# Attention-value products that load 128 stationary columns instead of 96

## The chip, the cores and the metric

One core of a Trainium2 chip runs the whole program. The metric is the time of one execution in device microseconds; lower is better. PE is TensorE, PEld its weight load, DVE is VectorE, ACT is ScalarE, POOL is GpSimd. Times are medians over several executions, and each experiment was timed in five rounds beside the kernel before on the same chip.

## The reference, cut to what matters

An attention layer is followed by an MLP. For each of 4 batches and 8 heads the sequence of 768 is cut into 8 blocks of 96. A doubly normalised 8x8 matrix mixes the blocks of k and v, then each block of q attends to its own mixed block:

```python
scores = scale * np.matmul(q_b, k_sb.transpose(0, 1, 2, 4, 3))   # 96 x 96 per head and block
scores = scores - np.max(scores, axis=-1, keepdims=True)
attn = np.exp(scores)
attn = attn / (np.sum(attn, axis=-1, keepdims=True) + 1e-09)
return np.matmul(attn, v_sb).reshape(B, H, S, D)                 # 96 x 96 times 96 x 64
...
tok = np.einsum('ts,bsd->btd', w_tok, a1)                        # 768 x 768 token product
u = x + lam * tok
ch = np.maximum(a2 @ w_ch1, 0.0) @ w_ch2                         # 512 -> 2048 -> 512
```

The change is in the last product of the attention, `attn @ v`. There are 4 x 8 x 8 = 256 of them, each with 96 rows of attention, 96 keys and 64 values, plus one column of ones in v that yields the row sums.

## The kernel before

The exponentials of a pair of heads and four blocks lie side by side in one tile `et`: 96 partitions (keys) by 2 x 4 x 96 columns (queries). The 96 query columns of one block are the stationary operand of a product; the 65 columns of `Vs` stream past. `et` is written by one ACT instruction:

```python
        et = att.tile([BLK, 2, 4, BLK], F16, name="et", tag="et", bufs=4)      # BLK = 96
        act.activation(et[:]..., sps[0:BLK]..., AF.Exp, scale=scale)
```

Batches 1 to 3 use `emit_pv`, and the scheduler mixes its products with those of the MLP of the batch before:

```python
    def emit_pv(b, h4, ets, x128, xs):
        for g in range(2):
            xps = psa([BLK, 4, 256], FT, "x_ps")
            for ii in range(4):
                i = 4 * g + ii
                for h2 in range(2):
                    pe.matmul(
                        xps[:, ii, h2 * GRP:h2 * GRP + D + 1], ets[g][:, h2, ii, :],
                        Vs[b % NV][:, (2 * h4 + h2) * NB + i, 0:D + 1],
                        start=True, stop=True,
                    )
            ...                             # DVE: reciprocal of the sums, multiply, into x128
```

Batch 0 uses `pv_tiles`, in a fixed order. Three blocks fill output rows 0 to 95 and thirds of a fourth block (32 columns each) fill rows 96 to 127, so that the token product can contract over 128 rows:

```python
        for rows, cols, i in ((slice(0, BLK), BLK, 0), (slice(BLK, 128), 32, 3)):
            for h2 in range(2):
                for ii in range(3):
                    vi = 3 * g + ii if i == 0 else 6 + g
                    lhsT = et[:, h2, ii, :] if i == 0 else et[:, h2, 3, 32 * ii:32 * ii + 32]
                    pe.matmul(xps[rows, h2, ii, 0:D + 1], lhsT, Vs[0][...], start=True, stop=True)
```

So 240 products load 96 columns (48 in batch 0, 192 later), and 48 load 32.

The softmax here doesn't subtract the row's maximum and nothing guards it: scores larger than these inputs give would overflow.

## Time and profile before

| | before |
|---|---|
| time, median (lowest to highest) | 271.24 us (271.13 to 271.33) |
| span of the profiled execution | 269.4 us |
| PE busy | 97% |
| attention-value products (x_ps) in the chain that ended last | 5.6% |
| start to start of a 96-column product, median of 240 | 45 ns |

The first lines are from the page of the kernel before: its part 1 (busy microseconds, share of the span, instructions) and two rows of part 2 (tenths busy, and granted clock in tenths, in 40 slices of the span).

```profile
PE 260.8 (97%) x2049; PEld 145.5 (54%) x2059; DVE 155.0 (58%) x333; ACT 126.0 (47%) x232; POOL 92.4 (34%) x100
...
PE   7899999999999999999999999999999999999993
...
PEclk9999999999999999999999999999999999999999
```

TensorE is busy from end to end at full clock. A busy PE is not yet a PE at its peak, because the ends of products are modelled. What a product costs is read from where the next one starts. The chain of waits that ended last, in order of time, gives this for whole groups of products (start, microseconds, what). Three of its lines from a later attention stretch of the kernel before:

```profile
130.88 0.71 PE x_ps L65 x16
131.59 1.30 PE h_ps L65 x8
...
140.06 0.35 PE x_ps L65 x8
```

Sixteen attention-value products take 0.71 us and eight take 0.35, about 44 ns each. Eight products of the MLP (128 stationary, 384 moving columns) take 1.30 us, 162 ns each. The groups of instructions by shape show the weight loads (PEld). After the bar stand busy microseconds and the mean duration of one in ns:

```profile
L65 PEld LDWEIGHTS <-W1p 128*128 128x128 bf16 x512 | 47.6, 98 | 30.3 <-issue 0.9
...
L65 PEld LDWEIGHTS <-et 96*96 96x96 f16 x240 | 14.3, 125 | 3.1 <-issue 0.3
```

The load of 96 columns lasts 125 ns and the larger load of 128 columns 98 ns. The duration includes latency that overlaps with other loads. The spacing of products has to be taken from the starts of single records. Over the whole trace, products with 128 stationary columns start 56, 162 and 216 ns apart for 128, 384 and 512 moving columns (medians): 0.417 ns per moving column plus 2.5. A product with 65 moving columns would then need 29.6 ns, and 45 ns were measured. Here the load is the longer of the two.

### The profile page before, as it was taken

Reading aid. Unit: us, or ns where it says so; the run is one execution under the profiler, and the core shown is the slowest. Engines: PE = TensorE matmul, PEld = TensorE weight load, DVE = VectorE, ACT = ScalarE, POOL = GpSimd, SP = SyncE. Lnnn points to the kernel's source line nnn. Section 1 sums busy time; section 2 is a strip of 40 time slices with the busy share of each in tenths; the row PEclk is TensorE's granted clock in tenths of the full one; section 3 lists DMA queues with packets and bytes.
Section 4 is the critical chain, followed back from the end, with each engine's and each line's share of the span. In section 5 each row is a group of like instructions: output and inputs, shape, how many; then the busy total and the mean of one; then the engine's idle time right before and its main releaser. Section 6 shows DMA issues by size and latency. Waiting matters only on the chain.

```text
span 269.4 us, 5147 instructions
## 1 busy us (share of the span) xinstructions
PE 260.8 (97%) x2049; PEld 145.5 (54%) x2059; DVE 155.0 (58%) x333; ACT 126.0 (47%) x232; POOL 92.4 (34%) x100
## 2 busy tenths in 40 slices
PE   7899999999999999999999999999999999999993
PEld 2467755565566444554565444654665445545542
DVE  6878688639567876722575966714575962042033
ACT  3376757642585312980365414970475305604600
POOL 8524689103574624007917225002409000000000
PEclk9999999999999999999999999999999999999999
DMA  6999999989999543499999342493200332012012
GB/s 80 181 208 249 207 211 207 210 197 113 193 171 163 106 93 97 117 83 83 208 202 137 61 99 79 117 104 55 79 2 2 78 78 78 2 39 78 2 39 78
DMA packets 62423, 30.88 MB, mean 115 GB/s; under 512 B 48888, under 2 KB 58112, under 8 KB 62400
## 3 DMA queue, kind: packets, MB, share of 16 engines
q0 software_dynamic: 23024, 15.60, 39.0%
q1 hardware_dynamic: 39376, 14.96, 33.4%
q8 instruction: 16, 0.26, 0.4%
q14 instruction: 7, 0.06, 0.1%
HBM read 32.78 MB, written 8.65 MB: 154 GB/s over the span
## 4 chain that ended last, share of the span: by engine, by line
PE 89%; ACT 4%; DVE 4%; issue 1%; DMA 1%; DVEq 0%; ACTq 0%
PE ch_ps L65 30%; PE h_ps L65 30%; PE tok_ps L65 12%; PE x_ps L65 6%; PE sc_ps L65 4%; ACT kT L65 2%; PE v_ps L65 2%; PE k_ps L65 1%; PE q_ps L65 1%; ACT et L65 1%; DVE csum L65 1%; DVE P_78 L65 1%; PE m_ps L65 1%; DVE rsum L65 1%; PE wtok_ps L65 1%
## 5 line engine op out<-in xcount | busy, mean ns | idle before, releaser
L65 ACT ACTIVATE hTa<-h_ps 128x384 bf16<-128x384 f32 x96 | 45.9, 492 | 70.9 <-PE h_ps L65 70.0
L65 PE MATMUL ch_ps<-W2p,hTa 128*128 128x512 bf16 (+2 forms) x290 | 66.0, 371 | 0.5
L65 PEld LDWEIGHTS <-W1p 128*128 128x128 bf16 x512 | 47.6, 98 | 30.3 <-issue 0.9
L65 DVE TENSOR_TENSOR ch_ps<-ch_ps,lamB 128x512 f32<-128x512 f32 (+2 forms) x25 | 16.9, 677 | 64.3 <-PE ch_ps L65 61.7
L65 PEld LDWEIGHTS <-hTa 128*128 128x128 bf16 x300 | 28.6, 98 | 32.4
L65 ACT ACTIVATE et<-sc_ps 96x768 f16<-96x768 f32 x32 | 24.9, 807 | 12.1 <-PE sc_ps L65 12.1
L65 PE MATMUL ch_ps<-W2p,hTb 128*128 128x512 bf16 (+2 forms) x100 | 25.0, 371 | 0.0
L65 PEld LDWEIGHTS <-w_tokT 128*128 128x128 f16 x180 | 14.8, 97 | 16.1
L65 DVE TENSOR_TENSOR tok_ps<-tok_ps,a1lB 128x512 f32<-128x512 f32 x24 | 16.6, 693 | 8.1 <-PE tok_ps L65 8.1
L65 DVE CAST kT<-k_ps 64x512 f16<-64x512 f32 x24 | 16.5, 687 | 3.4 <-PE k_ps L65 3.0
L65 PEld LDWEIGHTS <-et 96*96 96x96 f16 (+1 forms) x288 | 16.2, 120 | 3.4 <-issue 0.3
L65 ACT ACTIVATE hTb<-h_ps 128x384 bf16<-128x384 f32 x32 | 15.3, 498 | 3.8 <-PE h_ps L65 3.4
L65 PEld LDWEIGHTS <-hTb 128*128 128x128 bf16 x100 | 9.6, 98 | 10.9
L65 PEld LDWEIGHTS <-kT 64*96 64x96 f16 x256 | 8.6, 120 | 9.4 <-issue 3.6
L65 PE MATMUL sc_ps<-qT,kT 64*96 64x96 f16 x256 | 12.2, 213 | 0.2
L65 DVE RECIPROCAL recip<-x_ps 96x8 f32<-96x8 f32 (+1 forms) x32 | 6.0, 193 | 11.0 <-PE x_ps L65 10.6
L65 PE MATMUL h_ps<-a2T_2221,W1p 128*128 128x384 bf16 x64 | 12.2, 327 | 0.1
L65 PE MATMUL h_ps<-a2T_1506,W1p 128*128 128x384 bf16 x64 | 12.2, 327 | 0.1
L65 POOL DMA_DIRECT2D qn<-in_q_dram x12 | 10.8, 921 | 4.1 <-PE q_ps L65 3.4
L65 PE MATMUL h_ps<-a2T_792,W1p 128*128 128x384 bf16 x64 | 12.1, 327 | 0.0
L65 PE MATMUL h_ps<-a2T_2222,W1p 128*128 128x384 bf16 x64 | 12.1, 327 | 0.0
L65 PE MATMUL h_ps<-a2T_1507,W1p 128*128 128x384 bf16 x64 | 12.1, 327 | 0.0
(275 smaller groups left out, 381.8 us busy)
## 6 DMA issues: line engine op xcount, KB each, us to landing
out_dram<-ost SPq DMA_DIRECT2D x23, 192.0 KB, 2.2
vscr<-vA SPq DMA_DIRECT2D x6, 384.0 KB, 4.4
W1p<-in_moe_w_ch_dram POOLq DMA_DIRECT2D x4, 512.0 KB, 10.6
W2p<-in_moe_w_ch_dram POOLq DMA_DIRECT2D x4, 512.0 KB, 18.3
Vs_98<-vscr SPq DMA_DIRECT2D x4, 384.0 KB, 7.6
qn<-in_q_dram POOLq DMA_DIRECT2D x12, 128.0 KB, 5.9
out_dram<-ost SPq DMA_DIRECT2D x23, 64.0 KB, 2.0
wt_100<-in_moe_w_tok_dram POOLq DMA_DIRECT2D x1, 864.0 KB, 14.8
```

The source lines that it names most:

```text
L65: ins = getattr(self.eng, name)(*args, **kwargs)
```

## The change

The exponentials of the next block follow directly in `et`, so a load can simply run on for 32 more columns. The product then has 128 output rows. In batches 1 to 3 nobody reads rows 96 to 127; in batch 0 the 32-column products overwrite them later. The intent is a cheaper load for the same product. In batches 1 to 3 the last block of a tile has no successor and keeps 96 columns: 216 of 240 loads become 128 wide (48 and 168).

```diff
     def emit_pv(b, h4, ets, x128, xs):
         for g in range(2):
-            xps = psa([BLK, 4, 256], FT, "x_ps")
+            xall = psa([128, 4, 256], FT, "x_ps")
+            xps = xall[0:BLK]
+            flat = ets[g][:].rearrange("p a i x -> p (a i x)")
             for ii in range(4):
                 i = 4 * g + ii
                 for h2 in range(2):
+                    at = (h2 * 4 + ii) * BLK
+                    rows = min(128, 8 * BLK - at)
                     pe.matmul(
-                        xps[:, ii, h2 * GRP:h2 * GRP + D + 1], ets[g][:, h2, ii, :],
+                        xall[0:rows, ii, h2 * GRP:h2 * GRP + D + 1], flat[:, at:at + rows],
...
-        for rows, cols, i in ((slice(0, BLK), BLK, 0), (slice(BLK, 128), 32, 3)):
+        flat = et[:].rearrange("p a i x -> p (a i x)")
+        for rows, i in ((slice(0, 128), 0), (slice(BLK, 128), 3)):
...
-                    lhsT = et[:, h2, ii, :] if i == 0 else et[:, h2, 3, 32 * ii:32 * ii + 32]
+                    at = (h2 * 4 + ii) * BLK
+                    lhsT = flat[:, at:at + 128] if i == 0 else et[:, h2, 3, 32 * ii:32 * ii + 32]
```

## The prediction

> **What bounds the kernel now.** TensorE. The profile's first part has PE busy 260.8 of 269.4 us (97%), the second shows nine tenths in nearly every slice and a granted clock of 9 throughout, and the chain that ended last is 89% PE. The chain gives the attention-value products (x_ps) 5.6% of the span.
>
> **What one product costs.** From the starts of single instructions in the trace (a busy time hides it, for ends are modelled): a 96-column load with a 65-column product follows the last one after a median of 45 ns (240 of them). The product itself should stream in about 30 ns: the same 65 columns behind a 32-column load go at 29-32 ns, and products with 128 stationary columns run at 56 ns for 128 moving columns, 162 for 384, 216 for 512, which is 0.417 ns per column plus 2.5, so 29.6 ns at 65. So the load, not the product, sets the 45 ns. A 128-column f16 load is cheaper: the row sums (one moving column, 128 stationary) follow each other after 25 ns. The records agree: the 96-column load lasts 125 ns, the 128-column one 98. The Trainium skill, "TensorE: Matmul & The Clock Gate", section "Weight-path perf modes", says why: fast weight load is on when the number of weights is 128 and the type is not FP32, and was measured at about 2x.
>
> **What the change does.** It removes, adds and reorders no instruction; engines wait for the same things. 216 of the 240 loads go from 96 to 128 columns: 48 in batch 0, 168 in batches 1 to 3. In each group of eight there the last keeps 96 columns, as the tile ends. The product streams 65 columns as before; 32 more output rows cost no time. In batch 0 the surplus rows lie where the 32-column products write next; the switch to those (138 ns in the trace) stays.
>
> **Sum.** 45 - 30 = 15 ns times 216 = 3.2 us of PE time: 0.7 us in batch 0 (17.5 to 34.5 us), 0.84 us in each of the three later attention stretches. Nothing is added. The remaining 96-column load still exposes itself, and the first load of a group hides already under the longer product before it, so about 2.8 us.
>
> **How much is on the critical path.** Nearly all. Between 68 and 83 us PE never idles; the gaps around x_ps are mostly fixed switches of about 94 ns near the score products. A few waits could swallow some: x_ps on ACT's exponential (0.13 us once per stretch), and in batch 0 a 0.65 us wait for ACT's Vs copy, whose ACT work itself waits for PE's scores, so it should move along. I expect 2.6 us to reach the end: 268.6 us, -1.0%. Range 267.8 to 270.3.
>
> Chances: faster by over 2% 0.02, within 2% 0.96, slower by over 2% 0.02.
>
> **What would show it.** Loads of et 128 columns wide at about 98 ns in the groups; x_ps start to start near 30 ns; a group of eight followed by h_ps in about 0.26 instead of 0.36 us; the fourth part's x_ps share down from 5.6% to near 4.6%; starts of the token product (86.5, 145.9, 205.4 us) earlier by about 1.3, 2.0 and 2.7 us. Unchanged clock.
>
> **What would make it wrong.** If the fast load needs more than 30 ns beside a 65-column product, the saving shrinks towards nothing. If changing between fast and plain loads inside a group costs, half goes. If DVE or ACT pace batch 0, 0.3 to 0.5 us are lost. A slowdown would need a penalty for overwriting rows 96 to 127.

## The result, and the profile after

| | before | after |
|---|---|---|
| time, median (lowest to highest of 4 runs) | 271.24 us (271.13 to 271.33) | 268.71 us (268.56 to 270.01) |
| ratio, 95% interval | | 0.9916 (0.9894 to 0.9938) |
| x_ps in the chain that ended last | 5.6% | 4.7% |
| start to start of a widened product, median | 45 ns | 29 ns |

All ratios here are the mean time of one kernel's runs over that of the other's runs of the same rounds, so not quite the ratio of the medians. Executions over 1.5% slower than the fastest of the same kernel are left out of the means. The kernel became 2.5 us faster by the medians, 0.9%, and the interval of the ratio excludes 1.

The page of the changed kernel, the same rows:

```profile
PE 257.3 (96%) x2049; PEld 141.6 (53%) x2059; DVE 154.8 (58%) x333; ACT 125.8 (47%) x232; POOL 92.6 (35%) x100
...
PE   7799999999999999999999999999999999999993
...
PEclk9999999999999999999999999999999999999999
```

The groups of instructions by shape of the changed kernel, the loads of `et` alone (216 of the 240):

```profile
L65 PEld LDWEIGHTS <-et 96*128 96x128 f16 x216 | 9.4, 97 | 4.2 <-issue 1.2 <-DVE xs L65 0.7
```

The load moved a third more columns and got 28 ns shorter. The same three places of the chain in order of time:

```profile
129.64 0.51 PE x_ps L65 x16
130.15 1.30 PE h_ps L65 x8
...
138.23 0.27 PE x_ps L65 x8
```

Sixteen products went from 0.71 to 0.51 us, eight from 0.35 to 0.27, and the MLP products between them did not change. Single starts of one group of eight, in ns from the first of the eight to the first product after them (worked out from the records of the two traces; the last row is from experiment 1):

```
before      0  44  89 135 180 224 269 314 | 360
after       0  30  66  95 125 154 183 217 | 257     (the eighth still loads 96 columns)
112 columns 0  52 103 155 207 258 310 362 | 407     (the eighth loads 96)
```

Summed over the whole trace, start to next start, the 240 products took 11.46 us before and 8.46 us after (7.46 for the 216, 0.99 for the 24): 3.0 us less. The span shrank by 2.57, and 0.09 us of that was there before the first score product of batch 0 (17.99 us before, 17.90 after). So 0.5 us came back elsewhere. Laid over each other product by product (2049 records in each, in the same order), the two traces show where: from the attention of batch 1 on, the changed kernel is further ahead after each group of products, except at four places where it loses 0.11 us at one product. Here is one of them. First the timeline of the kernel before (start, us, engine, what, idle time before it and what ended that):

```profile
76.09 0.55 PE L65 MATMUL x_ps<-Vs_98,et 96*96 96x65 f16 x8
76.32 0.82 ACT L65 ACTIVATE et<-sc_ps 96x768 f16<-96x768 f32 x1
...
76.47 0.82 PE L65 MATMUL h_ps<-a2T_792,W1p 128*128 128x384 bf16 x4
...
77.19 0.51 PE L65 MATMUL x_ps<-Vs_98,et 96*96 96x65 f16 x8
```

And the same place in the timeline of the changed kernel:

```profile
75.24 0.43 PE L65 MATMUL x_ps<-Vs,et 96*128 96x65 f16 x8
...
75.47 0.81 ACT L65 ACTIVATE et<-sc_ps 96x768 f16<-96x768 f32 x1
75.50 0.82 PE L65 MATMUL h_ps<-a2T,W1p 128*128 128x384 bf16 x4
...
76.33 0.42 PE L65 MATMUL x_ps<-Vs,et 96*128 96x65 f16 x8
76.33 0.30 PEld L65 LDWEIGHTS <-et 96*128 96x128 f16 x7 [0.24 <-issue]
```

In both, the second group of products starts 0.05 us after ACT's exponential ends (76.32 + 0.82 = 77.14 and 77.19; 75.47 + 0.81 = 76.28 and 76.33). The work that PE has meanwhile, eight attention-value and four MLP products, became 0.12 us shorter, the exponential did not. PE is busy by the modelled ends, so the page's waits do not list this; it is seen only in the starts. Measured as the excess over 0.417 ns per column plus 2.5, the gaps before x_ps that ACT's exponential ended grew by 0.43 us in all (0.11 at each of the four places; at three of them the excess had been 15 ns or less before). In both kernels the product at such a place starts 49 to 52 ns after the exponential's end. The rest of the 0.5 us, under 0.1, is spread over gaps of a few ns.

### The profile page after: what moved, and what is told of

The parts are those of the page before. It is cut to its first block, busy times and chain, and to the rows that moved or that the text cites. A ratio compares the mean times of both kernels' runs of the same rounds, so it can differ in the third digit from the quotient of the medians.

```text
span 266.8 us, 5147 instructions
## 1 busy us (share of the span) xinstructions
PE 257.3 (96%) x2049; PEld 141.6 (53%) x2059; DVE 154.8 (58%) x333; ACT 125.8 (47%) x232; POOL 92.6 (35%) x100
## 4 chain that ended last, share of the span: by engine, by line
PE 89%; ACT 4%; DVE 4%; issue 1%; DMA 1%; DVEq 0%; ACTq 0%
PE ch_ps L65 31%; PE h_ps L65 30%; PE tok_ps L65 12%; PE x_ps L65 5%; PE sc_ps L65 4%; ACT kT L65 2%; PE v_ps L65 2%; PE k_ps L65 1%; PE q_ps L65 1%; ACT et L65 1%; DVE csum L65 1%; DVE P L65 1%; PE m_ps L65 1%; DVE rsum L65 1%; PE wtok_ps L65 1%
## 5 line engine op out<-in xcount | busy, mean ns | idle before, releaser
L65 PE MATMUL h_ps<-a2T,W1p 128*128 128x384 bf16 x512 | 93.4, 326 | 0.2
L65 POOL TENSOR_SCALAR u<-b1lB,rs 128x512 f32<-128x512 f32 x18 | 28.9, 1612 | 64.7 <-DVE ost L65 60.1
L65 PE MATMUL tok_ps<-x,w_tokT 128*128 128x512 f16 x144 | 32.1, 379 | 0.0
L65 POOL TENSOR_TENSOR u<-x,u 128x512 f32<-128x512 f16 x22 | 25.4, 1190 | 18.2 <-DVE x L65 17.3
L65 ACT CAST u<-u 128x512 f16<-128x512 f32 x24 | 14.8, 618 | 25.7 <-DVE u L65 25.7
L65 DVE TENSOR_TENSOR x<-x_ps,recip 96x512 f16<-96x512 f32 (+2 forms) x32 | 17.6, 554 | 0.9
L65 DVE TENSOR_TENSOR u<-tok_ps,u 128x512 f32<-128x512 f32 x24 | 16.4, 689 | 1.7
L65 DVE TENSOR_TENSOR ost<-ch_ps,u 128x512 f32<-128x512 f32 (+2 forms) x25 | 16.6, 665 | 0.6
L65 POOL DMA_DIRECT2D qn<-in_q_dram x18 | 15.4, 872 | 4.2 <-PE q_ps L65 3.4
L65 PEld LDWEIGHTS <-et 96*128 96x128 f16 (+2 forms) x288 | 12.4, 99 | 4.6 <-issue 1.2
```

Of the source, the lines that this page charges most:

```text
L65: ins = getattr(self.eng, name)(*args, **kwargs)
```

## The experiments

Theory A: only the full 128 columns get a fast weight load, and this shortens a product from load-bound to stream-bound. Rivals: a wider stationary operand or more written rows help by degrees (rival B of the first expectation); all plain loads take the same 45 ns (rival C); the saving sits in one of the two code paths only; any load of 96 columns costs the extra time, whatever product it feeds. A second question is where 0.5 us of the 3.0 went. All kernels gave the right result unless told otherwise. The kernel before measured 271.22, 271.18 and 271.22 us in the three sessions.

### 1. 112 columns

```diff
-                    rows = min(128, 8 * BLK - at)
+                    rows = 112 if at + 128 <= 8 * BLK else BLK
```

(and 112 in place of 128 in batch 0)

> 112 columns where the change has 128, in the same 216 loads. Theory A (only the full 128 columns get the fast load; a plain load costs 0.417 ns per column plus about 5, as 45 ns for 96 suggests): starts of these products 52 ns apart, records of the load longer than 125 ns, 216 times +7 ns = +1.5 us, so 272.7 us, slower than the kernel before. Rival B (a wider stationary operand helps by degrees, or it is the written rows 96 to 127 that help): between 268.7 and 271.2 us, near 270, spacing between 29 and 45 ns. Rival C (plain loads all take 45 ns whatever the width): 271.2 us.

Measured: 272.22 us (272.18 to 272.39), ratio 1.004 (1.0027 to 1.0053): slower than before by 1.0 us. The groups of instructions by shape of this run:

```profile
L65 PEld LDWEIGHTS <-et 96*112 96x112 f16 x216 | 14.8, 131 | 2.8 <-issue 0.3
L65 PEld LDWEIGHTS <-et 96*96 96x96 f16 x24 | 3.0, 125 | 0.0
```

The products start 52 ns apart. 112 columns cost more than 96, and 128 cost less than either. That rules out rivals B and C: width by degrees and more written rows don't help, and the cost of a plain load does rise with its columns. Widths between 112 and 128 were not tried. The size was smaller than the 1.5 us expected, since the first load of a group hides behind the longer product before it: the sum of starts grew by 1.25 us (12.71 against 11.46).

### 2 and 3. One half of the change at a time

Batch 0 alone, then batches 1 to 3 alone:

```diff
 e2, in emit_pv:   -  rows = min(128, 8 * BLK - at)     +  rows = BLK
 e3, in pv_tiles:  -  lhsT = flat[:, at:at + 128] ...   +  lhsT = flat[:, at:at + BLK] ...
```

> Only the 48 products of batch 0 widened, the 192 of later batches as before. If the saving is 15 to 16 ns per widened load: -0.7 us, 270.5 us. If batch 0 is paced by ACT and DVE: 271.0 us or more.

> Only the 168 products of batches 1 to 3 widened. Additive theory: 168 times 15 to 16 ns = 2.6 us of PE time, less some 0.5 us of waits for ACT's exponential that open behind the shorter groups, as the trace of the change shows: 269.2 us. Together with the run on batch 0 alone it should add up to the 2.5 us of the whole change within 0.3 us.

Measured: 270.63 us (ratio 0.9982, 0.9968 to 0.9995) and 269.29 us (0.9930, 0.9918 to 0.9943), that is 0.59 and 1.93 us under the kernel before of the same session. They add up to 2.52 us; the whole change had 2.53. Per widened load that is 12.3 ns in batch 0 and 11.5 later, of the 15 to 16 that a product in the middle of a group gains. The intervals of the two ratios are wide beside these numbers (batch 0 alone: 0.1 to 0.9 us), so a small disturbance of one by the other could hide in them. The saving sits in both paths, and nothing shows that they disturb each other.

### 4. All 240 loads

```diff
-        et = att.tile([BLK, 2, 4, BLK], F16, name="et", tag="et", bufs=4)
+        wide = et_bufs[len(et_of) % 4]          # four [96, 8 * 96 + 32] tiles, made and zero-padded once
+        et = wide[:, 0:8 * BLK].rearrange("p (a i x) -> p a i x", a=2, i=4)
...
-                    rows = min(128, 8 * BLK - at)
+                    rows = 128
```

> The exponentials get 32 padding columns (zeroed once, in four buffers made once), so that the last load of each group of eight is 128 wide too: 240 of 240. Theory A: the product after it follows after 29 ns instead of 42, 24 times 13 ns = 0.3 us: 268.4 us against 268.7. If a plain load in a row of fast ones cost more than itself: a larger gain, 0.6 us or more. If the new buffers disturb the order: slower.

Measured: 268.45 us (268.41 to 268.82), ratio 0.9903. The groups of instructions by shape:

```profile
L65 PEld LDWEIGHTS <-et 96*128 96x128 f16 x240 | 10.0, 97 | 4.3 <-issue 1.2 <-DVE xs L65 0.7
```

The product behind the last load of a group follows after 29 ns, and the sum of starts is 8.15 us instead of 8.46. The 0.3 us are there in the trace; by the ratios the run is not told apart from the change. A plain load in a row of fast ones costs its own extra time, and no more.

### 5 and 6. The thirds first in batch 0, and both refinements together

```diff
-        for rows, i in ((slice(0, 128), 0), (slice(BLK, 128), 3)):
+        for rows, i in ((slice(0, 128), 3), (slice(0, BLK), 0)):
...
-                    at = (h2 * 4 + ii) * BLK
-                    lhsT = flat[:, at:at + 128] if i == 0 else et[:, h2, 3, 32 * ii:32 * ii + 32]
+                    at = (h2 * 4 + ii) * BLK if i == 0 else (h2 * 4 + 2) * BLK + 32 * ii
+                    lhsT = flat[:, at:at + BLK] if i == 0 else flat[:, at:at + 128]
```

> Batch 0 only differs from the change: the 32-column products go first, as windows of 128 columns whose first 96 output rows are garbage, and then the 96-column products overwrite rows 0 to 95 with plain loads. This gives back the fast load of 48 products (48 times 15 ns = 0.7 us) and removes the narrow column tile, whose entry and exit cost 94 ns each in the trace of the change (8 groups, so up to 1.5 us, part of which stays where the score products follow). Expected: 0.3 to 0.8 us faster than the change, 268.1 us. Rival: the 94 ns belong to any change of operand, then 0.7 us slower, 269.4 us.

> The windowed order of batch 0 together with the padded exponentials (all 192 later loads 128 wide). If the two gains add: about 0.9 us under the change, 267.8 us.

Measured: 268.67 us (268.26 to 272.19, the longest of six at a granted clock of 0.986; ratio 0.9931) and 268.55 us (267.83 to 269.25, ratio 0.9902): no gain over the change, and none over the padding alone, that the intervals could tell. Yet PE's own work did shrink: the 288 products of the attention took 9.99 us from start to start, against 10.75 in the change. The narrow column tile had indeed cost an excess of 94 ns to enter and 96 to leave.

The traces show two things that ate it. The profiled execution of experiment 5 took 269.67 us, 1.0 us over the median of its runs, so it shows what that execution lost; what the others lost has no trace. In it PE waited for DVE, and DVE for the token weights from memory. The waits of PE and a line of the timeline:

```profile
PE wtok_ps L65 <- DVE wtp L65: 1.5, 1, 1.5
```

```profile
25.82 0.94 DVE L65 COPY wtp<-wt 128x1152 f16<-128x1152 f16 x2 [1.28 <-DMA wt<-in_moe_w_tok_dram]
```

The second part of that transfer landed at 25.31 us here, at 23.28 in the change's trace and at 23.95 in the trace before. It varies by 2 us between executions of programs that issue it within 0.3 us of each other, and a shorter batch 0 meets it earlier. In experiment 6 it landed in time, and the start of the token product gained 0.49 us over experiment 4; yet by 41 us all but 0.08 us of it was lost. The chain that ended last, of experiment 6 in this stretch, says why:

```profile
22.12 9.17 DMA W1p<-in_moe_w_ch_dram
31.29 0.28 issue
31.57 0.07 POOL W2p L65
31.65 0.68 issue
32.33 1.28 POOL a1lB L65
33.62 1.23 POOL b1lB L65
34.85 0.02 issue
34.87 1.41 DVE u L65 x2
...
39.31 1.23 ACT u L65 x2
40.54 0.05 issue
40.59 0.73 PE uT_ps L65 x10
```

POOL issues its last weight load only after an earlier one has landed (it waited 1.81 us for it in this trace), and POOL's two small products with lambda stand behind it in program order. DVE, ACT and at last PE wait for them. PE's gap at 40.59 us is 0.41 us longer than its product needs. The shorter batch 0 ran into this second chain.

### 7. The scores too

The same widening on the score products (on top of the change): 96 columns of k, 64 rows, two products side by side.

```diff
-                    sps[0:BLK, h2, ii, 0:BLK], kT[rows, h4 * NB + i, :], qT...
+                    sps[0:n, h2, ii, 0:BLK], kflat[rows, at:at + n], qT...     # n = 128, 96 for the last block
```

> The same widening on the score products (96 columns of k, 64 rows, two products side by side in two row tiles), on top of the change. There the pair already goes at 41 ns, which is what 96 moving columns take by themselves (96 times 0.417 plus 2.5 = 42.5). Theory A with the rule that a cheaper load helps only where the load is the longer of the two: no change, 268.7 us within 0.3. Rival: any 96-column load costs 15 ns more than a 128-column one: 128 pairs times 10 to 15 ns = 1.3 to 1.9 us faster, 267.1 us.

Measured: 268.78 us (268.53 to 270.05), ratio 0.9909, no change in time against the change. The loads in the groups by shape:

```profile
L65 PEld LDWEIGHTS <-kT 64*128 64x128 f16 x248 | 6.7, 94 | 9.5 <-issue 3.6 <-DVE kT L65 2.2 <-DVE x L65 1.8
```

The reasoning behind that expectation was nevertheless incomplete. The pair goes every 43 ns (45 before, so little is gained there), but the first pair after the switch to the half-height tiles (64 rows, one product in each half of the array) went on after 53 instead of 80 ns: there the load seems not to hide behind a running product. Over 32 groups of eight, the sum of starts fell from 10.08 to 8.98 us. In the trace 0.30 us of it went into the gaps before x_ps that end with the exponential. The profiled execution, 270.05 us, cannot tell where the rest went, because it also lost 2 us near 105 us: a pair of transposing DMAs landed late (DVE waited 3.78 us for them, 1.86 in the change's trace).

### 8. Exponentials in two halves

```diff
+        if b > 0:                      # two tiles [96, 4, 96], one exponential each; products in head order
```

> The change with each later exponential written to two tiles, one per head, so that the products wait for half an exponential only; 192 products in head order, 144 widened. Theory on the part of the gain that was given back (about 0.4 us: products now waiting longer for the exponential, because the shorter group ahead of it covers less of it): those waits of 0.12 to 0.17 us before x_ps go, while 24 loads fewer are fast (+0.35 us): 268.4 to 268.8 us, and no exposed wait of x_ps for ACT over 0.1 us. Rival: ACT's 4.5 us of added work delays the exponentials: 269.5 us or more.

Measured: 270.11 us (269.93 to 270.51), ratio 0.9962. The experiment did not do what it was made for: the first product of a group waits for both halves. In the trace its load starts when the first half ends, 0.50 us after the pair's start, but the product itself 0.05 us after the second half. So the wait was lengthened, not halved (0.88 us for the pair instead of 0.81). The rival's time came out. As a dose it is still of use. Against the change's trace the gaps before x_ps products behind an exponential grew at nine places (by 0.09 us at four, 0.16 at two and 0.02 at three) and shrank by 0.11 at two, 0.51 us net; 0.51 us went once before the transposes (at 40.6 us in the change's trace), behind POOL as in experiment 6; and the starts of the 288 products themselves sum to 0.46 us more, 24 of their loads being plain again. The timeline of this run at one of the nine:

```profile
76.39 0.88 ACT L65 ACTIVATE et<-sc_ps 96x384 f16<-96x384 f32 x2
76.40 0.82 PE L65 MATMUL h_ps<-a2T,W1p 128*128 128x384 bf16 x4
...
76.89 0.10 PEld L65 LDWEIGHTS <-et 96*128 96x128 f16 x1
...
77.33 0.44 PE L65 MATMUL x_ps<-Vs,et 96*128 96x65 f16 x8
77.33 0.33 PEld L65 LDWEIGHTS <-et 96*128 96x128 f16 x7 [0.34 <-issue]
```

Exponential's end at 77.27, products at 77.33. Here the load's idle time is 0.34 us; it was 0.24 in the change.

### 9 and 10. Shorter exponentials, before and after

Wrong results: later exponentials for one head only, in both kernels (which also got four fixed buffers for `et`, not shown in the cut). The check of the result would not have caught such an error.

```diff
-            et[:].rearrange(...), sps[0:BLK].rearrange(...), AF.Exp, scale=scale,
+            et[:, 0:heads].rearrange(...), sps[0:BLK, 0:heads].rearrange(...), AF.Exp, ...   # heads = 2 if b == 0 else 1
```

> Wrong result on purpose: the kernel before, with every exponential of batches 1 to 3 done for one head of the two only (0.50 instead of 0.81 us), so that the products' wait for it ends 0.3 us sooner. Partner of the next run; alone it should be 270.4 to 271.2 us, a little under the kernel before.

> Wrong result on purpose: the same on the changed kernel. If the 0.4 us that the change gave back went into longer waits for the exponential, then with this wait taken away from both, the change brings nearly all of its PE time: 2.9 to 3.1 us under the run before it, instead of 2.5. Rival (the give-back is elsewhere, in DVE, POOL or DMA): still 2.3 to 2.6 us.

Measured: 270.93 us (270.72 to 270.96) and 269.38 us (268.53 to 269.83), a difference of 1.55 us where the theory had 2.9 to 3.1 us and its rival 2.3 to 2.6. Experiment 9 came out within its expected range; for experiment 10 both forecasts missed. The built order is another one: at two places between 76 and 80 us one or two MLP products stand between two groups of eight, where the kernel before has four, probably because the scheduler knows that the exponential is shorter. The wait was not taken away. It stands, in experiment 10, at six products with a total loss of 0.65 us against experiment 9; of batch 0's gain (0.60 us in the change) only 0.13 us was left at the token product, and there the token weights landed late again (24.71 us); 0.36 us went in front of the transposes behind POOL. PE's saving itself was the same as ever, 3.05 us (11.50 to 8.46). So the pair doesn't isolate the exponential's share. In this one pair of executions all three waits took from the saving.

### 11 and 12. The second chain taken away, and everything together

On top of experiment 6, POOL's two products move ahead of its last weight load; then the scores of experiment 7 as well.

```diff
         for g in range(4):
+            if g == 3:
+                prep_affine()                    # was called later, after the scores of batch 0
             pool.dma_start(W2p[:, g * 4:(g + 1) * 4, :], w2v[:, g * 4:(g + 1) * 4, :])
```

> The windowed order plus the padded exponentials (which together measured no better than the padding alone), with POOL's two products of alpha1, beta1 and lambda moved ahead of its last weight load. Theory: batch 0's gain of 0.5 us was lost because DVE waits for POOL's b1lB, which stands behind a load that waits for a landing; PE then waits 0.4 us for ACT before the transposes near 40.6 us. With b1lB ready by 32.5 us instead of 34.8, that wait goes: 268.0 us, and no PE wait over 0.1 us near 40 us. Rival (paced by something else there): 268.5 us as before.

> The run before it with the score products' loads widened to 128 columns too, whose trace showed the first pair after each switch 28 ns sooner (0.03 us in each of 32 groups, 1.0 us of PE time) while the time did not move. If that gain was lost to the same POOL wait in batch 0: up to 0.3 us faster, 267.7 us. If it is lost to the exponential's wait in the later batches, as the scores lie ahead of it there: no difference from the run before it within 0.2 us.

Measured: experiment 11, 268.20 us (267.95 to 271.64), ratio 0.9905 with a wide interval (0.9869 to 0.9942), as one of its six runs was 3.4 us longer at a granted clock of 0.987. By the ratio it is not told apart from experiment 6 (0.9902); its median is 0.35 us lower. The trace is clearer. In experiment 6 the timeline of PE reads

```profile
40.06 0.28 PE L65 MATMUL uT_ps<-ident,u 128*128 128x128 f16 x2
40.59 0.73 PE L65 MATMUL uT_ps<-ident,u 128*128 128x128 f16 x10 [0.25 <-ACT u L65]
```

and in experiment 11

```profile
40.12 0.83 PE L65 MATMUL uT_ps<-ident,u 128*128 128x128 f16 x12
```

The wait is gone, and the next token product (85.00 us in experiment 6, 84.63 in 11) is 0.37 us earlier. Experiment 12 measured 267.21 us (267.16 to 267.68), ratio 0.9854 (0.9841 to 0.9866): 1.0 us under experiment 11 and 4.0 under the kernel before. The gain is larger than either of its two expectations. The two profiled executions differ by 0.7 us in span. Laid over experiment 11, experiment 12 gains 0.24 us in batch 0 and 0.14 to 0.15 us in each of the three later stretches. The gaps before x_ps that end with the exponential grew by another 0.27 us there, so a quarter of the 1.0 us of PE time went into that wait and the rest arrived. It beats both kernels, with the right result. Why experiment 7 showed none of this in its time is open: its one trace was 0.31 us ahead of the change's at the second token product before the late transposes, and its four other runs have no trace.

## Why the prediction was right

- **What bounds the kernel**: right. PE stayed busy at 96% and full clock, and time fell with PE's work.
- **The load, not the product, sets the 45 ns**: right, and shown by experiment 1: with 112 columns the spacing went to 52 ns and the time up, with 128 to 29 ns and down. The Trainium skill ("TensorE: Matmul & The Clock Gate", "Weight-path perf modes") gives the condition, fast weight load at exactly 128 weights of a type other than FP32, and the traces agree at 96, 112 and 128.
- **About 30 ns a product**: right, 29 measured. 0.417 ns per column plus 2.5 held for a length that no product behind a fast load had shown before.
- **Nothing added, nothing reordered**: right for the instructions.
- **The sum**: 2.8 us of PE time forecast, 3.0 measured. The deduction for the remaining 96-column loads and for the hidden first loads was a little too large.
- **How much reaches the end**: 2.6 us forecast, 2.5 measured. The term was mis-sized: the prediction lets 0.2 us go, 0.5 us went. It named the wait for ACT's exponential as one that could swallow some, at 0.13 us once a stretch; in the trace it grew by 0.43 us, at two places in the first of the three later stretches and at one in each of the others. That the end still came within 0.1 us is partly luck: the saving was forecast 0.2 us too small and the loss 0.3 us too small, and the two errors nearly cancel.
- **Batch 0 moves along**: right for the change: 0.68 us earlier at the token product, of which 0.60 was gained in batch 0 (0.7 forecast) and the rest was there before its first score product. It would not have been right for much more. Experiments 5, 6 and 10 show two limits close behind, a landing and POOL's order.
- **Marks in the profile**: the eight products took 0.27 us (0.26 forecast), the share 4.7% (4.6), the token products came 1.25, 1.90 and 2.57 us earlier (1.3, 2.0, 2.7).

In the one pair of traces the exponential's wait holds 0.43 of the 0.5 us. Experiment 8 shows that a longer exponential delays the x_ps products behind it. Experiment 10 failed to take the wait away, so that share is read from starts and not tested.

## What to carry to other kernels

When the moving operand is short, look at the spacing of starts rather than busy time: if it exceeds what the streamed columns need, the load may set the pace, and padding the stationary operand to the width of the fast load is worth a trial if the surplus outputs are unread or overwritten later; here the 32 more rows cost nothing that the starts show (29 ns a product). "Wider" is not the rule: 112 columns were worse than 96. And a saving in one place shortens what covers the latencies behind it, so check the waits after the shortened work, and the engines and landings that run beside it, before adding the next saving.

## What the Trainium skill lacked or had wrong

- "TensorE: Matmul & The Clock Gate", "LDWEIGHTS": it gives columns over 1.2 in ns, 80 ns for 96. Here plain loads sustained one every 45 ns for 96 columns and every 52 for 112, about 0.44 ns a column. The 125 and 131 ns of their records are latency that overlaps.
- The same page, "Weight-path perf modes": it gives about 2x for fast weight load. Here products with one moving column and a fast load of 128 columns each (the row sums) follow each other after 25 ns; plain loads of 128 columns would need some 59 ns (an estimate, continued from 45 and 52), so at least 2.3x in such a stream.
- The same page, "What overlaps and what doesn't": it says that loads overlap with products in flight only when the row group differs. Here products over all 128 rows with a fresh load each start 56 ns apart for 128 moving columns and 216 for 512, which leaves 2.5 ns beyond the streaming. The loads are hidden. Taken alone the sentence is too narrow; elsewhere the same page names a second case, a load into the background weight buffer, but no run here shows which case this is.
- "TensorEngine Tiling (Array Packing)", "Key Properties": it says that changing the tiling mode drains TensorE, without a figure. Entering or leaving the half-height tiles of the scores or the 32-column tile mostly cost 92 to 96 ns here beyond the product's own time, and behind such a switch a plain load of 96 columns is exposed by 27 ns more than a fast one (80 against 53 ns in the scores). The page says under "Restrictions" that column tiling disables fast weight load; for two row tiles the traces show it working (records of 94 instead of 120 ns in experiments 7 and 12).
- No page has it: the spread in landing of one transfer. The second part of the token weights landed between 23.28 and 25.31 us over the 14 traces here (of different programs), issued between 8.25 and 8.51.
